# Spreading operands over the partitions by TensorE instead of through DRAM, with a shorter plan at the front

## The chip, the cores and the metric

One core of a Trainium2 chip runs the whole program. The metric is the device time of one execution in microseconds (us). The engines are PE (TensorE; PEld is its weight load), DVE (VectorE), ACT (ScalarE), POOL (GpSimd) and SP (SyncE, which issues nearly all DMAs here). Each works through its own queue in order.

## What is computed

A delta-rule attention over 768 steps for 4 x 8 heads with a 40 x 40 state, then a mixture of experts (one expert of 8 for each of 3072 tokens), then a gated product of two matmuls and an output matmul. The attention, to which the change belongs:

```python
for t in range(S):                     # S = 768, batch 4, 8 heads, D = 40
    y[:, :, t] = np.einsum('bhd,bhde->bhe', rt, state)
    Sa = np.einsum('bhde,bhe->bhd', state, at)
    state_decay = state * wt[:, :, None, :] - np.einsum('bhd,bhe->bhde', Sa, bt)
    state = state_decay + np.einsum('bhd,bhe->bhde', vt, kt)
```

## The kernel before

The 768 steps are split into 12 chunks of 64 (c = 0 to 11). For each chunk some steps, the front, need no state:

- `cum` (L139 to L163): the cumulative products of w in tile `bf`, four scans on DVE (L151).
- `prod` (L165): the inputs `raw` times `bf` (L174, on DVE or POOL), each split into a high and a low float16 part, by ACT and by POOL: `ara` (a), `kb` (k and b), `arr` (r). Each result is stored to DRAM (`out`), as are `bf`'s first two rows (L197, `dg`) and a small decay factor (L205, `dds`).
- `fetch`, `rfetch`: `spread` (L213) reads them back so that the three 40-row groups of the partitions hold the high, low and high parts of the same rows (for a: high, high, low), which lets one 120-row matmul do a product of split numbers. The tiles are `a3`, `kb3`, `r3` (a, kb, r in the rows below) and `DT`.
- `gram` (L256): products of kb and a, one quarter (`g`) at a time, masked into `gm` by DVE (L257). `ztr` transposes kb into Z. `gtr` reads `dg` back into `dl` and transposes it on PE into `gt`, the scale of y.
- `invert` inverts 16 x 16 blocks on DVE, after a trip through DRAM (`tin`, `tl`) that regroups them; `twrite` and `tload` bring the result back by another one (`td`, `TT`); `merge` makes the 64 x 64 inverses out of them on PE, beginning with a transpose on DVE (L298).

The chain then carries the state: for each chunk and each of four blocks, x, u, S and S3 (parts C0 to C4), and the outputs n and y (O0 to O3). Many of these matmuls are float32 and 40 columns wide. Some are preceded by a matmul without use (`warm`, L359).

The source gives every step a due time in `PLAN` (L499): `gram=(5,-1.95,-1.8)` means five pieces that stand between 1.95 and 1.8 chunks ahead of their own. A scheduler then orders each engine's queue when the program is built, from these priorities and its own durations. PSUM tiles of the front steps share one pool, `pb`, with two buffers. The mixture of experts and the last stage follow; their weights begin to load when the last chunks free memory.

Of the kernel before, what the change touches and what calls it, by code (L numbers as in the profile page):

```python
# [10 lines left out]
F32 = mybir.dt.float32  # L11
F32R = mybir.dt.float32r
F16 = mybir.dt.float16
# [4 lines left out]
AF = mybir.ActivationFunctionType  # L18
ALU = mybir.AluOpType
# [4 lines left out]
def sub(ap, off, dims):  # L24

    return bass.AP(tensor=ap.tensor, offset=ap.offset+off, ap=[list(ap.ap[0])]+[list(d) for d in dims])
# [15 lines left out]
    d['vt']=v[:,::-1].reshape(12,128,4*160)[:NC].copy()  # L42
    return d

KB,R3,A3,NZ,GT=1,3,3,4,2
QN,QF=3,3
WARM=(0,256,256,256,256,512,256)
LAG,WHAT=12,'tl'
# [4 lines left out]
class Attn:  # L53
# [13 lines left out]
    def setup1(s):  # L67
        nc=s.nc; c=s.c
        if s.moe is None:
            s.idf=c.tile([128,128],F32,name="idf"); make_identity(nc,s.idf)  # L70
        else: s.idf=s.moe.idf
        s.idh=c.tile([128,128],F16,name="idh"); nc.vector.tensor_copy(s.idh,s.idf)
        s.tri=c.tile([128,64],F32,name="tri"); s.trg=c.tile([128,2,64],F32,name="trg")
        nc.gpsimd.memset(s.tri,1.0)
        for h in (0,1):
            v=s.tri[64*h:64*h+64]
            nc.gpsimd.affine_select(out=v,in_=v,compare_op=ALU.is_gt,fill=0.0,base=0,pattern=[[1,64]],channel_multiplier=-1)
        sc=-1.0/(AL*BE); ts=nc.vector.tensor_scalar
        for p in (0,1):
            ab=slice(64*p,64*p+64); ak=slice(64-64*p,128-64*p)  # L80
            nc.vector.tensor_copy(s.trg[ak,p],s.tri[ak])
            ts(out=s.trg[ab,p],in0=s.tri[ab],scalar1=sc,scalar2=None,op0=ALU.mult)
# [79 lines left out]
        s.load(c+1,0)  # L162
        yield  # L163
    def prod(s,c):
        nc=s.nc; V=nc.vector; d=s.ch[c]; raw=[d[('raw',n)] for n in range(5)]  # L165
        bf=d['bf']
        ar=[s.tile([128,2,6,128],F16,"ar"+n,f"ar{n}{c}",1) for n in "ar"]
        kb=s.tile([128,2,6,2,2,64],F16,"kb",f"kb{c}",KB)
        def out(t,n,w):
            dr=d['d'+n]=s.scr(n,[2,120,6,w],F16,c)  # L170
            nc.sync.dma_start(dr.rearrange("h r i t -> r h (i t)"),t[0:120])
        for (a,o) in ((2,2),(3,2),(1,0)):
            t=raw[a].rearrange("r (i h t) -> r h i t",h=2,t=32)
            (nc.gpsimd if c and a in s.PP else V).tensor_tensor(out=t,in0=t,in1=bf[:,o:o+2,:,o//2:o//2+32],op=ALU.mult)  # L174
            if a==1:
                src=raw[1].rearrange("r (i f) -> r i f",i=6)
                nc.scalar.activation(ar[0][:,0],src,AF.Copy)
                s.psub(ar[0][:,1],src,ar[0][:,0])
                out(ar[0].rearrange("r h i t -> r h (i t)"),"a",128)
            else:  # L180
                o0,ps=((64,64),(0,192))[a-2]
                src=sub(raw[a][:,0:1],0,[[128,6],[64,2],[1,64]])
                d0=sub(kb[:,0,0,0,0,0:1],o0,[[256,6],[ps,2],[1,64]]); d1=sub(kb[:,1,0,0,0,0:1],o0,[[256,6],[ps,2],[1,64]])
                nc.scalar.activation(d0,src,AF.Copy)
                nc.gpsimd.tensor_tensor(out=d1,in0=src,in1=d0,op=ALU.subtract)
                if a==3: out(kb.rearrange("r h i p s t -> r h (i p s t)"),"k",256)
            s.load(c+1,a)
            yield
        src=raw[4].rearrange("r (i f) -> r i f",i=6)
        V.tensor_scalar(out=raw[4],in0=raw[4],scalar1=RO,scalar2=None,op0=ALU.mult)  # L190
        nc.scalar.activation(ar[1][:,0],src,AF.Copy)
        s.psub(ar[1][:,1],src,ar[1][:,0])
        out(ar[1].rearrange("r h i t -> r h (i t)"),"r",128)
        s.load(c+1,4)

        dg=d['dg']=s.scr("g",[120,12,64],F32,c)
        for h in (0,1): nc.sync.dma_start(dg[:,:,32*h:32*h+32],bf[0:120,h,:,0:32])  # L197

        r32=s.tile([128,12],F32,"r32",f"r32{c}",2)
        V.tensor_copy(r32,bf[:,1,:,32])  # L200
        if c>0:
            dd=s.tile([128,12],F32,"dd",f"dd{c}",2); ip='r (i p) -> r i p'
            V.scalar_tensor_tensor(out=dd.rearrange('r (p i) -> r i p',p=2),in0=s.R32.rearrange(ip,p=2),scalar=1.0/(AL*KA),in1=bf[:,2,:,0].rearrange(ip,p=2),op0=ALU.mult,op1=ALU.mult)
            dds=s.dr.tile([2,120,6],F32,tag="dds",name=f"dds{c}")
            nc.sync.dma_start(dds.rearrange("p r i -> r p i"),dd[0:120].rearrange("r (p i) -> r p i",p=2))  # L205
            d['dds']=dds
        s.R32=r32
        d.update(kb=kb)
        yield

    def spread(s,t,dr,lo):
        for g in range(3):
            s.nc.sync.dma_start(t[40*g:40*g+40].rearrange("e (j i) t -> e j (i t)",j=3),dr[int(g==lo)].rearrange("(j e) i t -> e j (i t)",j=3))  # L213
    def rfetch(s,c):
        d=s.ch[c]
        r3=d['r3']=s.tile([128,18,128],F16,"r3",f"r3{c}",R3)
        s.spread(r3,d['dr'],1)
        yield
    def gtr(s,c):
        nc=s.nc; d=s.ch[c]  # L220
        da=s.tile([128,6,2,64],F32,"dl",f"dl{c}",1)
        nc.sync.dma_start(da[0:120].rearrange("r i a t -> r (i a t)"),d['dg'].rearrange("r i t -> r (i t)"))
        gt=d['gt']=s.tile([128,18,40],F32,"gt",f"gt{c}",GT)
        yield
        for hh in (0,1):
            pg=s.pst(f"pg{c}{hh}")
            n=4 if hh==0 else 2
            for i2 in range(n):
                tr=nc.tensor.transpose(pg[:,i2*120:i2*120+120], da[0:120,4*hh+i2].rearrange("p a t -> p (a t)"), s.idf[0:120,0:120])
                if i2==0: s.pin(tr)  # L230
            nc.scalar.activation(sub(gt[:,4*hh,0:1],0,[[240,3],[40,n],[1,40]]),sub(pg[:,0:1],0,[[40,3],[120,n],[1,40]]),AF.Copy)
            yield
    def fetch(s,c):
        nc=s.nc; d=s.ch[c]
        a3=s.tile([128,18,128],F16,"a3",f"a3{c}",A3)
        kb3=s.tile([128,18,2,128],F16,"kb3",f"kb3{c}",1)
        d.update(a3=a3,kb3=kb3)
        s.spread(a3,d['da'],2)
        yield
        s.spread(kb3.rearrange("e k p t -> e k (p t)"),d['dk'],1)  # L240
        yield
        if c>0:
            dds=d['dds']
            for p in (0,1):
                nc.sync.dma_start(s.DT[c%4][64*p:64*p+40].rearrange("e (j i) -> e j i",j=3),dds[p].rearrange("(j e) i -> e j i",e=40))
        yield

    def gram(s,c):
        nc=s.nc; d=s.ch[c]
# [225 lines left out]
        s.load_t(c); yield  # L475
    def run(s):

        for n in (0,2,3,1,4): s.load(0,n)
        ev=[]
        for c in range(s.NC):  # L480
            for nm,(n,a,b) in PLAN.items():
                g=s.part(int(nm[0]=='O'),int(nm[1]),(1,3) if nm=='O3' else range(4),c) if nm[0] in 'CO' else getattr(s,nm)(c)
                for i in range(n): ev.append((c+a+(b-a)*i/n,c,nm,g))
        g1=s.setup2()
        def once(f):
            f(); yield
        ev.append((SETUP[0],-1,'s1',once(s.setup1)))
        if s.moe is not None:
            ev.append((-.8,-1,'s3',once(lambda: s.moe.early_loads(s.tile([128,320],F32,"y","ymoe",2)))))
            ev.append((s.NC-1.4,-1,'s4',once(lambda: s.moe.zero(s.tile([128,320],F32,"y","yzero",2)))))  # L490
        for i in range(6): ev.append((SETUP[1]+i*SETUP[2],-1,'s2',g1))
        ev.sort(key=lambda e:e[0])
        last={}
        for e in ev: last[e[1:3]]=e
        for e in ev:
            next(e[3],0)
            if last[e[1:3]] is e:
                for _ in e[3]: pass
SETUP=(-3.04,-2.3,.05)  # L499
PLAN=dict(cum=(5,-3.456,-2.956),prod=(5,-2.906,-2.556),fetch=(3,-2.45,-2.3),gram=(5,-1.95,-1.8),tread=(1,-1.68,-1.67),ztr=(6,-1.85,-1.5),invert=(30,-1.5,-1.13),twrite=(1,-1.1,-1.09),tload=(1,-0.92,-0.91),gtr=(3,-0.9,-0.3),merge=(9,-0.7,-0.2),vpre=(4,-0.796,-0.088),rfetch=(1,0.05,0.06),C0=(4,-0.081,-0.071),C1=(4,-0.047,0.086),C2=(4,0.191,0.462),O0=(4,0.315,0.573),C3=(4,0.462,0.734),C4=(4,0.463,0.735),O1=(4,0.586,0.858),O2=(4,0.718,0.96),O3=(2,0.96,1.028))  # L500


NT=3072; NTI=24; D=320; E=8; F=1024; FF=1536; NB=13; NBT=21
# [2 lines left out]
class Moe:  # L506
# [463 lines left out]
    def moe2(s,ctx,st):  # L970
# [3 lines left out]
        def fetch(g):  # L974
# [7 lines left out]
            for k in range(3):  # L982
# [3 lines left out]
                s.xsplit(XH,XL,t,k)  # L986
            return XH,XL
        X=fetch(0)
        for g in range(6):
            XH,XL=X  # L990
# [71 lines left out]
```

## Time and profile before

| | us |
|---|---|
| median of 3 runs (lowest, highest) | 1581.28 (1576.04, 1589.54) |
| the profiled execution | 1577.47 |
| its span in the trace | 1575.7 |
| PE busy in the span | 1198.2 |
| DVE, ACT, POOL busy | 716.3, 530.3, 470.9 |

Busy time is the time in which an engine has an instruction under way; matmuls are pipelined, so the mean time of one is longer than its share of a row of them. Idle time of an engine costs something only where the end waits for it. The rows below are copied from the profile's page and from answers of the trace.

### The profile page before, as it was taken

The page shows a single profiled execution, that of the slowest core. Times are in us where ns is not written, and L with a number is a line of the kernel's source. Part 1 is how long each engine was busy: PE and PEld are TensorE (multiplying, and loading weights), DVE is VectorE, ACT ScalarE, POOL GpSimd, SP SyncE. Part 2 cuts the span into 40 slices and gives each one's busy share as a digit, 9 for nine tenths or more (in the row PEclk, how much of TensorE's full clock was granted, in tenths as well). Part 3 has the DMA queues.
Part 4 walks back from the last instruction along what each step waited for, and adds up shares of the span by engine and source line. Part 5 has one row for each costly group of instructions (what it writes and reads, how often), then busy time and mean ns, then how long its engine had stood idle before and what let it go on. Part 6 is the DMA issues. An engine that isn't in the chain of part 4 may idle for free. (4 is left out here: it accounts for less than half of the span.)

```text
span 1575.7 us, 34604 instructions
## 1 busy us (share of the span) xinstructions
PE 1198.2 (76%) x14569; PEld 1043.3 (66%) x14569; DVE 716.3 (45%) x1485; ACT 530.3 (34%) x1068; POOL 470.9 (30%) x434
## 2 busy tenths in 40 slices
PE   0111678955766877698987788887878999999998
PEld 0011567744655666587876687877867888989888
DVE  6552652533333333133324529999989321222211
ACT  5111434321524414343444124545423122131221
POOL 3533421321121301110114206656445232242221
PEclk9999976555756757757765798999989999999999
DMA  6888445454344343423232116777532000100000
GB/s 176 235 211 237 104 128 138 102 150 118 84 111 98 79 105 91 104 63 85 55 104 83 43 45 185 215 213 208 175 95 73 19 18 17 34 9 25 1 17 17
DMA packets 200117, 160.48 MB, mean 102 GB/s; under 512 B 128465, under 2 KB 168209, under 8 KB 199953
## 3 DMA queue, kind: packets, MB, share of 16 engines
q1 hardware_dynamic: 197553, 149.99, 35.8%
q0 software_dynamic: 2400, 8.20, 1.9%
q8 instruction: 116, 1.90, 0.5%
q14 instruction: 48, 0.39, 0.1%
HBM read 113.87 MB, written 44.27 MB: 100 GB/s over the span
## 5 line engine op out<-in xcount | busy, mean ns | idle before, releaser
L807 PE MATMUL ab<-X2H,abh 128*128 128x512 f32 x432 | 171.1, 398 | 4.3 <-DVE pr L997 3.9
L788 POOL TENSOR_TENSOR pL<-pr,pH 128x512 fp32r<-128x512 f32 x72 | 93.4, 1297 | 242.7 <-ACT pH L790 242.5
L807 PE MATMUL ab<-X2H,abl 128*128 128x512 f32 x432 | 121.6, 389 | 0.0
L997 DVE TENSOR_TENSOR pr<-ab,sa 128x512 f32<-128x512 f32 x72 | 49.6, 690 | 149.5 <-PE ab L807 149.5
L807 PE MATMUL ab<-X2L,abh 128*128 128x512 f32 x288 | 112.9, 394 | 0.0
L807 PE MATMUL ph<-XHb,w1h 128*128 128x256 f32 x312 | 89.7, 311 | 29.4 <-DVE hL L874 28.0
L256 PEld LDWEIGHTS <-kb 120*128 120x128 f16 x384 | 25.5, 124 | 130.6 <-issue 117.6
L256 PE MATMUL g<-a,kb 120*128 120x64 f16 x384 | 29.8, 232 | 102.9 <-DMA a<-da 70.7
L807 PEld LDWEIGHTS ab<-X2H,abh 128*128 128x128 f32 x432 | 82.1, 190 | 23.3 <-DVE pr L997 6.1
L790 ACT ACTIVATE pH<-pr 128x512 fp32r<-128x512 f32 x72 | 45.6, 633 | 144.0 <-DVE pr L997 132.4
L807 PEld LDWEIGHTS ab<-X2H,abl 128*128 128x128 f32 x432 | 81.1, 188 | 16.9
L1007 PE MATMUL po<-wol,pH 128*128 128x320 f32 x288 | 89.7, 312 | 1.5 <-POOL wol L788 1.5
L1007 PE MATMUL po<-woh,pH 128*128 128x320 f32 x288 | 89.5, 312 | 0.2 <-ACT woh L951 0.2
L788 POOL TENSOR_TENSOR w1l<-wr,w1h 128x512 fp32r<-128x512 f32 x51 | 71.1, 1408 | 59.9 <-ACT w1h L828 38.1
L1007 PE MATMUL po<-woh,pL 128*128 128x320 f32 x288 | 88.8, 311 | 0.0
L807 PEld LDWEIGHTS ph<-XHb,w1h 128*128 128x128 f32 x312 | 65.2, 210 | 35.6 <-DVE hL L874 29.5
L120 POOL TENSOR_TENSOR Q<-Qf,Q 128x320 f16<-128x320 f32 x48 | 38.0, 793 | 150.5 <-ACT Q L428 150.5
L996 ACT ACTIVATE sa<-ab 128x512 f32<-128x512 f32 x72 | 43.0, 597 | 113.5 <-PE ab L807 113.0
L174 POOL TENSOR_TENSOR raw<-raw,bf 128x768 f32<-128x768 f32 x22 | 38.8, 1764 | 131.8 <-DVE bf L151 48.0
L377 PE MATMUL x<-Qf,gm 64*64 64x40 f32 x768 | 57.2, 292 | 20.1 <-DVE Qf L354 20.1
L151 DVE TENSOR_TENSOR_SCAN bf<-raw,D 128x396 f32<-128x396 f32 x48 | 51.1, 1085 | 39.9 <-DMA dg<-bf 31.0
L884 PE MATMUL po<-w2h,hH 128*128 128x320 f32 x208 | 65.8, 319 | 2.9 <-ACT hH L873 2.9
(309 smaller groups left out, 3238.4 us busy)
## 6 DMA issues: line engine op xcount, KB each, us to landing
raw<-ct SPq DMA_DIRECT2D x48, 384.0 KB
kb<-dk SPq DMA_DIRECT2D x36, 360.0 KB
wr<-moe_w SPq DMA_DIRECT2D x40, 320.0 KB
wr<-moe_w SPq DMA_DIRECT2D x40, 256.0 KB
dk<-kb SPq DMA_DIRECT2D x12, 720.0 KB
a<-da SPq DMA_DIRECT2D x36, 180.0 KB
r<-dr SPq DMA_DIRECT2D x36, 180.0 KB
wr<-moe_w SPq DMA_DIRECT2D x40, 128.0 KB
```

Source lines behind the costliest of these rows:

```text
L120: def psub(s,out,a,b): s.nc.gpsimd.tensor_tensor(out=out,in0=a,in1=b,op=ALU.subtract)
L151: V.tensor_tensor_scan(o,i,d1.rearrange("p i t -> p (i t)"),0.0,ALU.mult,ALU.add)
L174: (nc.gpsimd if c and a in s.PP else V).tensor_tensor(out=t,in0=t,in1=bf[:,o:o+2,:,o//2:o//2+32],op=ALU.mult)
L256: nc.tensor.matmul(pg[:,(q*2+p)*64:(q*2+p)*64+64], d['kb3'][0:120,k,p], d['a3'][0:120,k,64*p:64*p+64], start=True,stop=True)
L377: mm(o(px,q,p),gm[r,k0+q,p],Q[r,p,q],start=not S,stop=not S or q==3)
L788: def psub(s,L,a,H): s.nc.gpsimd.tensor_tensor(out=L,in0=a,in1=H,op=ALU.subtract)
L790: s.nc.scalar.activation(H,src,AF.Copy)
L807: for i,(a,b) in enumerate(l): mm(o,a,b,start=(i==0),stop=(i==7))
L884: nc.tensor.matmul(po,a[:,m,tk],b[:,m],start=(k==0 and m==0 and n==0),stop=(k==3 and m==1 and n==2))
L996: sa=w.tile([128,512],F32,tag="sa",name=f"sa{g}{m}"); nc.scalar.activation(sa,pp[0],AF.Copy)
L997: pr=w.tile([128,512],F32,tag="pr",name=f"pr{g}{m}"); V.tensor_tensor(out=pr,in0=pp[1],in1=sa,op=ALU.mult)
L1007: nc.tensor.matmul(po,a[:,m,tk],b[:,m],start=(n==0),stop=(n==35)); n+=1
```

## The change

The stores of `ara`, `kb`, `arr`, `bf` and the decay factor and all reads of them are gone. In their place `spread` multiplies the stored halves by a constant selection matrix `sps` (two accumulating matmuls for a piece of up to 512 columns, first the high and then the low part) into a `pb` buffer, and ACT and DVE take turns in copying the piece to `kb3`, `a3` or `r3`. `gtr` regroups `bf` by a copy on POOL and transposes that. The decay factor is brought to its partitions by six small float32 matmuls. The scaling and splitting of r moves out of `prod` into `rprep`, 0.3 chunks ahead of the chunk's own time, and `r3` has one buffer instead of three. In the plan `cum` begins 2.75 chunks ahead instead of 3.456, `gtr` moves to the front, and the steps from `gram` on keep their times.

```diff
-KB,R3,A3,NZ,GT=1,3,3,4,2
+KB,R3,A3,NZ,GT=1,1,3,4,4
...
+        s.sps=c.tile([128,2,2,3,120],F16,name="sps"); nc.gpsimd.memset(s.sps,0.0)
+        for y,lo in ((0,2),(1,1)):
+            for g in range(3):
+                nc.vector.tensor_copy(s.sps[:,y,int(g==lo),:,40*g:40*g+40],s.idh[:,0:120].rearrange("p (j e) -> p j e",j=3))
...
-            nc.sync.dma_start(dr.rearrange("h r i t -> r h (i t)"),t[0:120])
...
-        dg=d['dg']=s.scr("g",[120,12,64],F32,c)
-        for h in (0,1): nc.sync.dma_start(dg[:,:,32*h:32*h+32],bf[0:120,h,:,0:32])
...
-            nc.sync.dma_start(dds.rearrange("p r i -> r p i"),dd[0:120].rearrange("r (p i) -> r p i",p=2))
+            pd=s.pst(f"pd{c}")
+            for j in range(3):
+                for p in (0,1): nc.tensor.matmul(pd[64*p:64*p+40,6*j:6*j+6],s.idf[0:120,40*j:40*j+40],dd[0:120,6*p:6*p+6],start=True,stop=True)
+            for p in (0,1): nc.scalar.activation(s.DT[c%4][64*p:64*p+40],pd[64*p:64*p+40,0:18],AF.Copy)
...
-    def spread(s,t,dr,lo):
-        for g in range(3):
-            s.nc.sync.dma_start(t[40*g:40*g+40].rearrange("e (j i) t -> e j (i t)",j=3),dr[int(g==lo)].rearrange("(j e) i t -> e j (i t)",j=3))
+    def spread(s,dst,src,y,w,nm):
+        nc=s.nc; n0=512//w; n=0
+        for j in range(3):
+            m=6 if j<2 else 4; st=n0 if m%n0==0 else 3
+            for i in range(0,m,st):
+                ps=s.pst(f"sp{nm}{j}{i}"); o=ps[0:120,0:st*w]
+                for h in (0,1): nc.tensor.matmul(o,s.sps[0:120,y,h,j],src[0:120,h,i:i+st].rearrange("r i t -> r (i t)"),start=h==0,stop=h==1)
+                d=dst[0:120,6*j+i:6*j+i+st]; o=o.rearrange("r (i t) -> r i t",i=st)
+                if n%2: nc.vector.tensor_copy(d,o)
+                else: nc.scalar.activation(d,o,AF.Copy)
+                n+=1
+                yield
...
-        nc.sync.dma_start(da[0:120].rearrange("r i a t -> r (i a t)"),d['dg'].rearrange("r i t -> r (i t)"))
+        nc.gpsimd.tensor_copy(da.rearrange("r i p (h t) -> r h (i p) t",h=2),bf[:,0:2,:,0:32])
...
-PLAN=dict(cum=(5,-3.456,-2.956),prod=(5,-2.906,-2.556),fetch=(3,-2.45,-2.3),gram=(5,-1.95,-1.8),tread=(1,-1.68,-1.67),ztr=(6,-1.85,-1.5),invert=(30,-1.5,-1.13),twrite=(1,-1.1,-1.09),tload=(1,-0.92,-0.91),gtr=(3,-0.9,-0.3),merge=(9,-0.7,-0.2),vpre=(4,-0.796,-0.088),rfetch=(1,0.05,0.06),C0=(4,-0.081,-0.071),C1=(4,-0.047,0.086),C2=(4,0.191,0.462),O0=(4,0.315,0.573),C3=(4,0.462,0.734),C4=(4,0.463,0.735),O1=(4,0.586,0.858),O2=(4,0.718,0.96),O3=(2,0.96,1.028))
+PLAN=dict(cum=(5,-2.75,-2.56),gtr=(3,-2.55,-2.35),prod=(4,-2.5,-2.26),spr=(13,-2.25,-1.97),gram=(5,-1.95,-1.8),tread=(1,-1.68,-1.67),ztr=(6,-1.85,-1.5),invert=(30,-1.5,-1.13),twrite=(1,-1.1,-1.09),tload=(1,-0.92,-0.91),merge=(9,-0.7,-0.2),vpre=(4,-0.796,-0.088),rprep=(1,-0.3,-0.29),rspr=(5,0.06,0.3),C0=(4,-0.081,-0.071),C1=(4,-0.047,0.086),C2=(4,0.191,0.462),O0=(4,0.315,0.573),C3=(4,0.462,0.734),C4=(4,0.463,0.735),O1=(4,0.586,0.858),O2=(4,0.718,0.96),O3=(2,0.96,1.028))
```

In the rows that follow a name ends with the piece, the chunk and a serial number: `tin0_355` is chunk 0's tin, `kb31` chunk 1's kb3, `raw23` input 2 of chunk 3, `spk310` a piece of k's spread for chunk 3, `x10` the x of chunk 1, block 0.

On SP, in the fill, these stand from the first chunk's tin to its read tl, before:

```order
L263 DMA tin0_355<-gm0_282 16x16x16 x8
L213 DMA kb31_424<-dk1_351 40x3x1536 x3
L133 DMA raw23_505<-ct 128x768
L171 DMA dk2_548<-kb2_501 120x2x1536
L133 DMA raw33_550<-ct 128x768
L245 DMA DT2_218<-dds2_619 40x3x6
L213 DMA a31_423<-da1_369 40x3x768 x3
L171 DMA dr2_608<-arr2_500 120x2x768
L133 DMA raw43_610<-ct 128x768
L245 DMA DT2_218<-dds2_619 40x3x6
L213 DMA r31_1845<-dr1_389 40x3x768
L269 DMA tl0_364<-tin0_355 128x256
```

and these now:

```order
L138 DMA raw03_741<-wt 128x794
L138 DMA raw22_437<-ct 128x768
L138 DMA raw32_453<-ct 128x768
L264 DMA tin0_378<-gm0_320 16x16x16 x8
L138 DMA raw12_467<-ct 128x768
L270 DMA tl0_387<-tin0_378 128x256
```

Ten rows between tin0 and tl0 became one, a load.

On DVE, ahead of the first transpose of the first merge, before:

```order
L174 TENSOR_TENSOR raw34_1081<-raw34_1081,bf4_1449 128x2x12x32
L190 TENSOR_SCALAR raw44_1156<-raw44_1156 128x768
L151 SCALAR_TENSOR_TENSOR bf5_2308<-raw05_1667,D0_127 128x396 x2
L157 RECIPROCAL rr5_2309<-bf5_2308 128x12
...
L159 TENSOR_SCALAR D1_128<-rr5_2309 128x12
L151 SCALAR_TENSOR_TENSOR bf5_2308<-raw05_1667,D1_128 128x396
L174 TENSOR_TENSOR raw35_1935<-raw35_1935,bf5_2308 128x2x12x32
L298 STREAM_TRANSPOSE T11_209<-TT0_207 128x512
```

and now:

```order
L212 CAST kb32_971<-spk222_1017 120x512
L156 SCALAR_TENSOR_TENSOR bf4_2152<-raw04_1373,D1_145 128x396
L164 TENSOR_SCALAR D1_145<-rr4_2153 128x12
L212 CAST a32_970<-spa203_1069 120x384
L156 SCALAR_TENSOR_TENSOR bf4_2152<-raw04_1373,D1_145 128x396
L299 STREAM_TRANSPOSE T11_201<-TT0_199 128x512
```

Before, the scans of chunks 0 to 5 (24), eight products and five scalings of r stand ahead of that transpose; now it is the scans of chunks 0 to 4 (20), six products, two scalings and 17 evictions of spreads.

On PE, in the x step of chunk 1, before:

```order
L373 MATMUL x10_1690<-S300_1383,a31_423 64x40
L256 LDWEIGHTS kb33_1454
L256 MATMUL g131_1874<-a33_1453,kb33_1454 128x64
...
L359 LDWEIGHTS sel_270
L359 MATMUL g132_1896<-sel_270 128x512
...
L377 MATMUL x10_1690<-Qf10_1458,gm1_475 64x40
L330 MATMUL p110_1413<-TT1_208,P1b0_210 64x32 x16
```

and now:

```order
L378 MATMUL x10_1860<-Qf10_1575,gm1_564 64x40 x5
L210 LDWEIGHTS sps_127
L210 MATMUL spk310_1805<-kb3_1511,sps_127 120x512
L210 LDWEIGHTS sps_127
L210 MATMUL spk310_1805<-kb3_1511,sps_127 120x512
L378 MATMUL x10_1860<-Qf10_1575,gm1_564 64x40 x3
L371 LDWEIGHTS zh_298
L371 MATMUL x11_1880<-sel_296,zh_298 128x160
L374 LDWEIGHTS a31_493
```

Where pieces of chunk 3's gram stood between the matmuls of x, pairs of chunk 3's spread stand now, and its gram comes behind x. All spreads of k and a for chunks 0 to 2 stand ahead of the first merge's matmuls or just behind their first ones.

## Rows read from the trace of the kernel before

**Rows 1.** The page's 40 slices of the span: PE busy, granted clock, in tenths.
```profile
PE   0111678955766877698987788887878999999998
PEclk9999976555756757757765798999989999999999
```
**Rows 2.** Answers by tile: min/median/max ns, then first and last start in us.
```profile
L257 DVE TENSOR_TENSOR gm<-g,trg x48: 630/692/693, 51.2 to 729.0; 128x512 f32<-128x512 f32 x48
L276 DVE TENSOR_TENSOR tA<-tl,I x12: 382/383/1662, 87.3 to 766.3; 128x256 f32<-128x256 f32 x12
L298 DVE STREAM_TRANSPOSE T<-TT x12: 699/702/711, 142.2 to 801.5; 128x512 f32<-128x512 f32 x12
L453 DVE SCALAR_TENSOR_TENSOR y<-y,gt x48: 308/325/327, 230.8 to 871.3; 128x160 f32<-128x160 f32 x48
```
**Rows 3.** Stretches: length, busy us of PE, PEld, DVE, ACT, POOL; granted clock; DMA share; GB/s.
```profile
0.00:142.00 142.00, 11.43 (x140) 7.70 (x140) 72.98 (x141) 38.32 (x52) 54.60 (x43) 1.00 0.79 207
142.00:872.00 730.00, 553.16 (x10768) 464.08 (x10768) 273.21 (x720) 273.95 (x606) 162.15 (x183) 0.67 0.42 104
735.00:872.00 137.00, 118.78 (x2153) 100.02 (x2152) 48.34 (x135) 59.57 (x133) 35.95 (x52) 0.63 0.30 82
560.00:600.00 40.00, 37.69 (x537) 32.10 (x537) 12.19 (x45) 12.56 (x31) 3.41 (x5) 0.50 0.34 73
526.00:541.00 15.00, 12.16 (x228) 9.91 (x226) 2.37 (x6) 10.17 (x23) 4.11 (x6) 0.96 0.29 62
1300.00:1350.00 50.00, 50.00 (x247) 42.78 (x246) 10.67 (x16) 14.47 (x25) 14.60 (x12) 1.00 0.06 15
```
**Rows 4.** Waits from 0 to 142 us: who for whom, us in total, times, longest.
```profile
PE g L256 <- DMA a<-da: 70.7, 2, 45.7
DVE raw L174 <- DMA raw<-ct: 17.8, 2, 10.3
DVE bf L151 <- DMA dg<-bf: 14.7, 1, 14.7
```
**Rows 5.** The same from 142 to 872 us.
```profile
ACT arr L191 <- DMA dr<-arr: 48.7, 3, 19.5
DVE raw L190 <- DMA raw<-ct: 40.8, 4, 18.5
PE g L256 <- DMA kb<-dk: 27.8, 3, 11.7
PE S L359 <- ACT Qf L389: 16.5, 1, 16.5
```
**Rows 6.** Groups by line over the span: busy us, mean ns | idle before.
```profile
L151 DVE TENSOR_TENSOR_SCAN bf<-raw,D 128x396 f32<-128x396 f32 x48 | 51.1, 1085 | 39.9 <-DMA dg<-bf 31.0 <-POOL raw L174 5.3 <-DMA raw<-wt 3.3
L996 ACT ACTIVATE sa<-ab 128x512 f32<-128x512 f32 x72 | 43.0, 597 | 113.5 <-PE ab L807 113.0 <-ACT pH L790 0.4
L257 DVE TENSOR_TENSOR gm<-g,trg 128x512 f32<-128x512 f32 x48 | 32.6, 687 | 55.6 <-PE g L256 55.2
L359 PE MATMUL g<-sel 128*128 128x512 f16 x48 | 26.0, 549 | 18.8 <-DVE gm L257 11.8 <-DVE sel L113 3.9 <-ACT Z L343 2.1
L581 PE MATMUL lg<-wgt,xt 128*128 128x8 f32 x96 | 22.3, 342 | 0.7 <-ACT xt L578 0.7
L174 DVE TENSOR_TENSOR raw<-raw,bf 128x768 f32<-128x768 f32 x14 | 20.5, 1474 | 21.3 <-DMA raw<-ct 17.8 <-ACT kb L184 3.3
L1008 DVE COPY yo<-po 128x320 f32<-128x320 f32 x24 | 11.7, 491 | 104.4 <-PE po L1007 104.4
L190 DVE TENSOR_SCALAR raw<-raw 128x768 f32<-128x768 f32 x12 | 7.6, 635 | 59.5 <-DMA raw<-ct 59.5
```
**Rows 7.** The chain that ended last: start us, us, what.
```profile
1307.79 32.67 PE ab L807 x144
```
**Rows 8.** PE's groups from 560 to 600 us, and then from 526 to 541 us.
```profile
L386 PE MATMUL u<-X,TT 64*64 64x40 f32 x64 | 4.3, 307 | 0.0
L386 PE MATMUL u<-X,TT 64*64 64x40 f32 x48 | 2.3, 229 | 0.0
```

More of the change, by code (lines that the diff above doesn't have):

```diff
@@ L164, in prod @@
     def prod(s,c):
-        nc=s.nc; V=nc.vector; d=s.ch[c]; raw=[d[('raw',n)] for n in range(5)]
+        nc=s.nc; V=nc.vector; d=s.ch[c]; raw=[d[('raw',n)] for n in range(4)]
         bf=d['bf']
-        ar=[s.tile([128,2,6,128],F16,"ar"+n,f"ar{n}{c}",1) for n in "ar"]
+        ar=s.tile([128,2,6,128],F16,"ara",f"ara{c}",1)
         kb=s.tile([128,2,6,2,2,64],F16,"kb",f"kb{c}",KB)
-        def out(t,n,w):
-            dr=d['d'+n]=s.scr(n,[2,120,6,w],F16,c)
-            nc.sync.dma_start(dr.rearrange("h r i t -> r h (i t)"),t[0:120])
+        d.update(kb=kb,ar=ar)
         for (a,o) in ((2,2),(3,2),(1,0)):
@@ L176, in prod @@
                 src=raw[1].rearrange("r (i f) -> r i f",i=6)
-                nc.scalar.activation(ar[0][:,0],src,AF.Copy)
-                s.psub(ar[0][:,1],src,ar[0][:,0])
-                out(ar[0].rearrange("r h i t -> r h (i t)"),"a",128)
+                nc.scalar.activation(ar[:,0],src,AF.Copy)
+                s.psub(ar[:,1],src,ar[:,0])
             else:
@@ L185, in prod @@
                 nc.gpsimd.tensor_tensor(out=d1,in0=src,in1=d0,op=ALU.subtract)
-                if a==3: out(kb.rearrange("r h i p s t -> r h (i p s t)"),"k",256)
             s.load(c+1,a)
             yield
[L189 to L194, printed above, removed]
-        dg=d['dg']=s.scr("g",[120,12,64],F32,c)
-        for h in (0,1): nc.sync.dma_start(dg[:,:,32*h:32*h+32],bf[0:120,h,:,0:32])
         r32=s.tile([128,12],F32,"r32",f"r32{c}",2)
@@ L203, in prod @@
             V.scalar_tensor_tensor(out=dd.rearrange('r (p i) -> r i p',p=2),in0=s.R32.rearrange(ip,p=2),scalar=1.0/(AL*KA),in1=bf[:,2,:,0].rearrange(ip,p=2),op0=ALU.mult,op1=ALU.mult)
-            dds=s.dr.tile([2,120,6],F32,tag="dds",name=f"dds{c}")
-            nc.sync.dma_start(dds.rearrange("p r i -> r p i"),dd[0:120].rearrange("r (p i) -> r p i",p=2))
-            d['dds']=dds
+            pd=s.pst(f"pd{c}")
+            for j in range(3):
+                for p in (0,1): nc.tensor.matmul(pd[64*p:64*p+40,6*j:6*j+6],s.idf[0:120,40*j:40*j+40],dd[0:120,6*p:6*p+6],start=True,stop=True)
@@ L207, in prod @@
+            for p in (0,1): nc.scalar.activation(s.DT[c%4][64*p:64*p+40],pd[64*p:64*p+40,0:18],AF.Copy)
         s.R32=r32
-        d.update(kb=kb)
         yield
-    def spread(s,t,dr,lo):
-        for g in range(3):
-            s.nc.sync.dma_start(t[40*g:40*g+40].rearrange("e (j i) t -> e j (i t)",j=3),dr[int(g==lo)].rearrange("(j e) i t -> e j (i t)",j=3))
[L214 to L217, printed above, removed]
+    def spread(s,dst,src,y,w,nm):
[10 more added lines that the diff above has]
+                yield
@@ L218, in rfetch, with rprep, rspr @@
+    def rprep(s,c):
+        nc=s.nc; raw=s.ch[c]['raw',4]
+        rr=s.ch[c]['rr']=s.tile([128,2,6,128],F16,"arr",f"arr{c}",1)
+        src=raw.rearrange("r (i f) -> r i f",i=6)
+        nc.vector.tensor_scalar(out=raw,in0=raw,scalar1=RO,scalar2=None,op0=ALU.mult)
+        nc.scalar.activation(rr[:,0],src,AF.Copy)
+        s.psub(rr[:,1],src,rr[:,0])
+        s.load(c+1,4)
         yield
+    def rspr(s,c):
+        r3=s.ch[c]['r3']=s.tile([128,18,128],F16,"r3",f"r3{c}",R3)
+        yield from s.spread(r3,s.ch[c]['rr'],1,128,f"r{c}")
@@ L219, in gtr @@
     def gtr(s,c):
-        nc=s.nc; d=s.ch[c]
+        nc=s.nc; d=s.ch[c]; bf=d['bf']
         da=s.tile([128,6,2,64],F32,"dl",f"dl{c}",1)
-        nc.sync.dma_start(da[0:120].rearrange("r i a t -> r (i a t)"),d['dg'].rearrange("r i t -> r (i t)"))
+        nc.gpsimd.tensor_copy(da.rearrange("r i p (h t) -> r h (i p) t",h=2),bf[:,0:2,:,0:32])
+        yield
         gt=d['gt']=s.tile([128,18,40],F32,"gt",f"gt{c}",GT)
-        yield
         for hh in (0,1):
@@ L228, in gtr, with spr @@
             for i2 in range(n):
-                tr=nc.tensor.transpose(pg[:,i2*120:i2*120+120], da[0:120,4*hh+i2].rearrange("p a t -> p (a t)"), s.idf[0:120,0:120])
-                if i2==0: s.pin(tr)
+                nc.tensor.transpose(pg[:,i2*120:i2*120+120], da[0:120,4*hh+i2].rearrange("p a t -> p (a t)"), s.idf[0:120,0:120])
             nc.scalar.activation(sub(gt[:,4*hh,0:1],0,[[240,3],[40,n],[1,40]]),sub(pg[:,0:1],0,[[40,3],[120,n],[1,40]]),AF.Copy)
             yield
-    def fetch(s,c):
-        nc=s.nc; d=s.ch[c]
+    def spr(s,c):
+        d=s.ch[c]
         a3=s.tile([128,18,128],F16,"a3",f"a3{c}",A3)
@@ L237, in fetch @@
         d.update(a3=a3,kb3=kb3)
[L238 to L246, printed above, removed]
+        yield from s.spread(kb3.rearrange("e k p t -> e k (p t)"),d['kb'].rearrange("r h i p s t -> r h i (p s t)"),1,256,f"k{c}")
+        yield from s.spread(a3,d['ar'],0,128,f"a{c}")
     def gram(s,c):
@@ L476, in run @@
     def run(s):
-        for n in (0,2,3,1,4): s.load(0,n)
+        for n in (0,2,3,1): s.load(0,n)
         ev=[]
@@ L487, in run @@
         ev.append((SETUP[0],-1,'s1',once(s.setup1)))
+        ev.append((-1.7,-1,'s5',once(lambda: s.load(0,4))))
         if s.moe is not None:
```

## The prediction

> **What bounds the kernel now.** I read the slices of the span first, to see where TensorE (PE) idles and at which granted clock [rows 1]. PE does almost nothing in the first four slices, is then busy for 55 to 90% at a clock of mostly 0.5 to 0.7 until about slice 22, and nearly full at 0.9 or more behind it. The change touches the attention alone, and the last y tile ends at 871 us [rows 2]; everything after it (704 us) I carry over unchanged.
>
> The stretches [rows 3] cut the attention in two. From 0 to 142 us PE is busy for 11.43 us: this is the fill, which ends with the first transpose of the merge at 142.2 us [rows 2]. From 142 to 872 us PE is busy for 553.16 of 730 us, 0.758 of the time, while DVE, ACT and POOL have 273, 274 and 162 us. So PE is the engine that limits this part, with 177 us of waiting in it. In the last stretch, where no front work is left, its share is 118.78 of 137, 0.867; from 560 to 600 us it is 0.942, at half clock.
>
> Who was waited for comes third. In the fill [rows 4] PE waits 70.7 us for tile a on its way back from DRAM, in two pieces; DVE waits 17.8 us for raw inputs at the products and 14.7 us because `bf` can't be overwritten before its copy to DRAM is out. From 142 us on [rows 5] PE waits 27.8 us for kb from DRAM and 16.5 us behind ACT, whose queue stood 48.7 us in all at `arr`, an operand still being written out; DVE stood 40.8 us at the scaling of r.
>
> **The change part by part.**
>
> *DRAM trips removed.* Per chunk the writes of a, k, r, g and dds and their reads go; the waits in the last paragraph that name da, dk, dr and dg go with them. The raw loads and the four trips of the inversion (tin, tl, td, TT) stay.
>
> *The fill.* In before 91 us lie between the first gram result (51.2 us) and the merge (142.2 us), with the first inversion at 87.3 us [rows 2]. The order of SP shows why a part of that can go: between tin0 and its read tl0 stood spreads, operand stores and loads; one load is left. DVE is what remains. Ahead of its first merge transpose it drops four scans (x 1.085), three scalings of r (x 0.635) and two products (x 1.474), 9.2 us in all, and gets 17 evictions of spreads and six small copies [rows 6]. DVE shows no eviction of a 120x512 spread: it lies between 0.491 us (a 128x320 copy from PSUM) and 0.687 us (the 128x512 gram result from PSUM); I take 0.65, nearer the row of that width. That is 11.1 us, with 1 us for the small copies (an estimate). DVE's busy time until the merge goes from 72.98 to 75.9 us. I add the 17.8 us of waiting for raw inputs at products, which stay, and drop the others: 94 us, a saving of 48 us. Bounds: if all of the 91 us stays behind a gram at 45 us, the merge starts at 136 us (6 saved); if DVE never waits, at 76 (66 saved).
>
> *PE's new work.* A chunk's spreads are 16 matmuls of 512 columns for k, and 8 of 384 and 2 of 512 each for a and r: 16384 columns, as much as 32 matmuls of 512. Those of k and a for chunks 0 to 2 (order of PE) stand ahead of the first merge, where PE idles anyway. Behind it are left 9 chunks of k and a and 12 of r, 312 matmuls of 512. Back to back such a matmul takes 32.67/144 = 0.227 us [rows 7] in a stretch with a granted clock of 1.00 [rows 3]: 70.8 us. The upper end is the warming matmul of the same width, 0.549 us from start to end [rows 6]: 171 us. At the clock of this stretch, 0.67, it is 70.8/0.67 = 106 us, which I take, since these matmuls stand among the others. The small product for the decay, 6 float32 matmuls a chunk of 6 columns, has no row; the nearest is the 128x8 float32 one with 0.342 us [rows 6], and below it nothing where the pieces overlap. I take 0.2 us x 54 = 11 us. g's transposes were there before. PE's busy time after the merge: 553 + 106 + 11 = 670 us.
>
> *ACT, DVE, POOL.* Eighteen evictions a chunk, ten on ACT at 0.597 us (128x512 from PSUM [rows 6]) and eight on DVE at 0.65, are 72 and 62 us over twelve chunks; with 274 and 273 of 730 us they stay under half. POOL's copy of g, 128x768, lies on an engine that is busy for 162 of 730 us. I cost these at nothing in the sum: PE's time covers them. If the cover is gone, PE waits for a free `pb` buffer (there are two), and this is a rival.
>
> *The clock.* The same matmul u takes 307 ns at a granted clock of 0.50 and 229 ns at 0.96 [rows 8, 3], so a stretch at the full level (2.4 GHz instead of 1.2) costs a quarter less. From 560 to 600 us PE is busy for 94% and still has the half level, with narrow float32 matmuls (40 columns) as its main work; at 526 to 541 us, with 81%, it has the full one. How far spreads of 512 columns lift it no row of before shows. Bounds: nothing, and 0.85 as the mean. I take a small step, 0.67 to 0.73: half-level time goes from 0.66 to 0.54 of it, 0.12 x 670 x 0.25 = 20 us less, 650 us. The Trainium skill ("TensorE: Matmul & The Clock Gate", Part 1) says that the throttled clock is the default and activity releases it. By that, dense spreads lift it more than I take, and the time is that of the first rival; the 94% busy stretch at 0.50 shows that being busy alone doesn't do it.
>
> *The waiting that is left.* PE's share was 0.867 where nothing came through DRAM for it and no filler was left. Now spreads of a chunk ahead stand between x, u and y (order of PE), and they need no result of the step before. I take 0.88, a little over the tail and under the 0.942: 650/0.88 = 739 us.
>
> *Sum.* 94 + 739 = 833 us to the end of the attention, against 872: 39 us less. The profiled execution took 1577.5 us, so 1538; it lies 3.8 us under the median of 1581.3, and I say **1540 us**.
>
> **Rivals.**
>
> *The clock rises.* With a mean of 0.85 the half level has 0.30 of the time instead of 0.66: 0.36 x 670 x 0.25 = 60 us less, 610/0.88 + 94 = 787, 85 us under before: 1493 us. For it: dense f16 columns are the new work, 14.5 us of them at the half level in a chunk of some 60 us. Against it: they stand in pairs among the same narrow matmuls.
>
> *Given back.* PE gets 117 us more work and nothing is filled: at the tail's 0.867 and an unchanged clock 670/0.867 + 94 = 867 us, 5 under before, 1573 us. With the fill hardly shorter (136 us) and 0.88 it is 650/0.88 + 136 = 875, 1581 us. The trips were then hidden by the front that ran ahead. For it: of the 177 us in which PE waits, the two waits above are only 44. Against it: the fill's 131 idle us are in the rows.
>
> *Slower: evictions hold PE.* Every spread needs a free `pb` buffer, and ACT and DVE take the eviction in their order, behind chain steps that themselves wait for PE. Each chunk has 18 such pieces where gram and its transposes had 9. Break-even is a PE share of 670/(872 - 94) = 0.861 at the old clock, just below the tail's, and at 0.844 the kernel is 1% slower. Half way between 0.867 and the 0.758 of before, 0.81, it is 827 + 94 = 921 us, 49 more: 1627 us. The Trainium skill ("TensorEngine Tiling (Array Packing)", PSUM Bottleneck) warns that evacuation may become the bottleneck when TensorE does more, and advises using both engines, as is done here. For the rival: ACT's queue already stood still for tens of us. Against: most of that was at `arr`'s store, which goes.
>
> **How the numbers follow.** Forecast (1515 to 1565 us) 0.40; the clock rises 0.20; given back 0.18; slower 0.22. About 1% is what a measurement of this kernel can tell from no change, so faster (under 1565) has 0.60, the same 0.18, slower (over 1597) 0.22. The range must hold the rising clock and the milder half of the slower case: 1478 to 1620, which leaves out some 0.06 below and 0.12 above.
>
> **What would show it.** Right: the first merge transpose starts between 76 and 110 us; no wait of PE for kb or a by DMA; PE busy about 650 us behind the merge at a clock over 0.7 and a share of 0.86 to 0.92; the last y at about 833 us; 704 us behind it. The clock rival shows as a mean granted clock over 0.8 there; the given-back one as a merge after 125 us, or a share at 0.867 with the clock at 0.67; the slower one as PE waiting at the spread matmuls for ACT or DVE, tens of us in total. I am wrong outright if PE's idle time moves to a wait that I don't name, such as the raw loads, which now come fewer chunks ahead, or the inversion's trips.

## The result, and the profile after

The changed kernel takes **1498.74 us** (median, 1491.13 to 1501.97) against 1582.74 of the kernel before on the same chip, a ratio of 0.946 with a 95% interval of 0.941 to 0.952: 84 us faster. The forecast was 1540 with a range of 1478 to 1620. The direction and the range hold; the gain is twice the 41 us that were forecast (1581 to 1540), and it is near the time of the rival in which the clock rises (1493).

The page's slices of the changed kernel, in the columns of [rows 1]:

```profile
PE   2678988969999797799988877778698999999998
PEclk9756586975757798797656989999899999999999
```

The empty slices at the left are gone, and the stretch of the attention has more digits of 7 to 9 in its clock than [rows 1], with 5 and 6 still between them.

First and last starts of four instructions, by tile:

```profile
L258 DVE TENSOR_TENSOR gm<-g,trg x48: 677/692/693, 44.8 to 679.5; 128x512 f32<-128x512 f32 x48
L277 DVE TENSOR_TENSOR tA<-tl,I x12: 381/404/1217, 57.1 to 692.2; 128x256 f32<-128x256 f32 x12
L299 DVE STREAM_TRANSPOSE T<-TT x12: 680/711/712, 92.5 to 729.0; 128x512 f32<-128x512 f32 x12
L454 DVE SCALAR_TENSOR_TENSOR y<-y,gt x48: 285/325/326, 160.0 to 794.2; 128x160 f32<-128x160 f32 x48
```

Against [rows 2] the first merge starts at 92.5 instead of 142.2 us, and the last y comes at 794 instead of 871. Between gram and the first inversion lie 12 us instead of 36, and from there to the merge 35 instead of 55.

The stretches, with the columns of [rows 3] (length, busy us of PE, PEld, DVE, ACT, POOL, granted clock, DMA share, GB/s):

```profile
0.00:92.00 92.00, 43.40 (x254) 24.79 (x255) 68.79 (x149) 44.57 (x73) 40.86 (x37) 0.84 0.39 98
92.00:795.00 703.00, 623.04 (x11219) 479.03 (x11217) 295.48 (x814) 327.40 (x728) 183.88 (x198) 0.72 0.25 61
795.00:1500.00 705.00, 629.84 (x3663) 567.37 (x3661) 376.64 (x626) 218.44 (x410) 258.86 (x212) 0.96 0.27 79
```

Of the 77 us by which the attention is shorter, 50 are the fill and 27 the part behind the merge. PE does 70 us more in that part (623 against 553) and still ends it sooner, since it waits for 80 us there instead of 177. What follows the attention takes 705 us against 704.

The waits behind the merge, as in [rows 5]:

```profile
POOL raw L177 <- DMA raw<-ct: 67.0, 11, 11.1
DVE T L299 <- DMA TT<-td: 66.0, 9, 14.2
ACT kb L213 <- PE spk L210: 54.0, 17, 6.0
DVE r L212 <- PE spr L210: 39.1, 16, 6.4
PE g L360 <- DVE gm L258: 23.7, 3, 10.2
```

No DMA stands among the long waits of PE any more. The DMAs that are waited for are the raw loads and the inversion's trips, by POOL and DVE. At the spreads the evicting engines wait for PE; PE itself has no wait ahead of a spread matmul there. Its largest wait, 23.7 us in all at gram (`g`) for the mask `gm` by DVE, is one that the prediction doesn't name.

### The profile page after: what moved, and what is told of

Its sections match the earlier page's. It is cut to its first block, busy times and chain, and to the rows that moved or that the text cites. A ratio compares the mean times of both kernels' runs of the same rounds, so it can differ in the third digit from the quotient of the medians.

```text
span 1500.2 us, 35616 instructions
## 1 busy us (share of the span) xinstructions
PE 1296.3 (86%) x15133; PEld 1071.2 (71%) x15133; DVE 740.9 (49%) x1587; ACT 590.4 (39%) x1210; POOL 483.6 (32%) x447
## 5 line engine op out<-in xcount | busy, mean ns | idle before, releaser
L210 PEld LDWEIGHTS <-sps 120*120 120x120 f16 x432 | 58.4, 165 | 58.8 <-issue 48.0
L210 PE MATMUL spk<-kb,sps 120*120 120x512 f16 x192 | 74.8, 502 | 25.9 <-POOL kb L187 9.3
L125 POOL TENSOR_TENSOR Q<-Qf,Q 128x320 f16<-128x320 f32 x48 | 42.9, 895 | 95.8 <-ACT Q L429 89.1
L187 POOL TENSOR_TENSOR kb<-raw,kb 128x768 f16<-128x768 f32 x24 | 40.7, 1718 | 89.8 <-ACT kb L186 77.1
L334 POOL MEMSET TT<- 32x512 f32 x24 | 12.5, 521 | 177.1 <-PE p L331 138.4
L809 PE MATMUL ph<-XLb,w1h 128*128 128x256 f32 x208 | 57.6, 303 | 10.4 <-DVE XLb L861 10.4
```

Of the source, the lines that this page charges most:

```text
L125: def psub(s,out,a,b): s.nc.gpsimd.tensor_tensor(out=out,in0=a,in1=b,op=ALU.subtract)
L210: for h in (0,1): nc.tensor.matmul(o,s.sps[0:120,y,h,j],src[0:120,h,i:i+st].rearrange("r i t -> r (i t)"),start=h==0,stop=h==1)
L809: for i,(a,b) in enumerate(l): mm(o,a,b,start=(i==0),stop=(i==7))
```

## The experiments

Two theories were left to tell apart for the part behind the merge: that a spread costs its columns at the clock as it is (columns), and that dense columns raise the clock and pay for themselves (clock). For the fill it was the path (no trips) against the plan (a front that runs less far ahead). The first four kernels below share their runs of the kernel before; so do the next four, and so do the last three. Across these groups the ratio to the kernel before compares better than the times do.

### The plan without the path

```diff
-cum=(5,-3.456,-2.956),prod=(5,-2.906,-2.556),fetch=(3,-2.45,-2.3)
+cum=(5,-2.75,-2.56),prod=(5,-2.5,-2.26),fetch=(3,-2.25,-1.97)
```

> The kernel before with the shorter plan alone: cum, prod and fetch get the due times of the changed kernel, operands still go through DRAM. Theory path (the trips were what was waited for; the plan only orders DVE's queue): the first merge moves from 142 to between 115 and 135 us, PE waits longer than 28 us for kb and a by DMA behind it, and the time is 1560 to 1610 us. Rival plan (the gain comes from a front that no longer runs six chunks ahead): merge at about 95 us, 1500 to 1530 us.

It took 1560.5 us, ratio 0.991 (0.988 to 0.995). The first merge, by tile, and PE's and ACT's longest waits for DMAs behind it:

```profile
L298 DVE STREAM_TRANSPOSE T<-TT x12: 698/711/712, 143.1 to 780.6; 128x512 f32<-128x512 f32 x12
...
ACT arr L191 <- DMA dr<-arr: 45.0, 4, 13.0
PE g L256 <- DMA kb<-dk: 15.5, 2, 13.6
PE g L256 <- DMA dr<-arr: 8.5, 1, 8.5
```

The time lies in the range of theory path, the mechanism does not: the merge doesn't move at all (143.1 us), and the waits for kb don't grow. DVE's wait for raw inputs at the products of the fill stays too (18.5 us, 17.8 in [rows 4]). The plan alone is worth about 1%, all of it behind the merge.

### The path without the plan

```diff
-cum=(5,-2.75,-2.56),gtr=(3,-2.55,-2.35),prod=(4,-2.5,-2.26),spr=(13,-2.25,-1.97)
+cum=(5,-3.456,-2.956),gtr=(3,-2.95,-2.85),prod=(4,-2.906,-2.556),spr=(13,-2.45,-2.0)
```

> The changed kernel with the front's old due times (cum from 3.456, prod from 2.906, spreads from 2.45 chunks ahead; gtr follows cum). Theory path: trips stay away, so the part behind the merge keeps its length (700 us, PE share 0.88); the first merge comes later, at 105 to 130 us, since DVE takes scans of more chunks first: 1510 to 1540 us. Rival plan: 1560 us or more.

It took **1454.0 us**, ratio 0.923 (0.917 to 0.930), less than either theory allowed and less than the changed kernel itself. By tile the first merge starts at 91.6 us. The part behind it:

```profile
92.00:748.00 656.00, 577.67 (x11198) 449.76 (x11199) 305.02 (x809) 325.56 (x722) 189.27 (x198) 0.77 0.25 64
```

So the 50 us of the fill come from the path alone: 143 us with the trips, 92 without them, whatever the plan. My expectation that an earlier front would hold up the merge was wrong. And the shorter plan costs time on the new path: behind the merge it has the same work and the same share of PE (0.881 here, 0.886 there), but a clock of 0.72 instead of 0.77.

### Each spread matmul twice

```diff
-for h in (0,1): nc.tensor.matmul(o,...,start=h==0,stop=h==1)
+for h in (0,1,0,1): nc.tensor.matmul(o,...,start=h==0,stop=h==1)
```

> The changed kernel with each spread matmul done twice into the same PSUM buffer (the second pair starts the sum anew), evictions unchanged. Theory columns (PE limits, a spread costs its columns at the clock as it is): 312 more matmuls of 512 behind the merge are 71 us at the full clock, 98 at 0.72, 111 at PE's share of 0.886: 1600 to 1620 us with a granted clock of 0.70 to 0.74 behind the merge. Rival clock (dense columns raise the clock and so pay for themselves in part): granted clock over 0.78 there, 1520 to 1570 us.

It took 1520.3 us, ratio 0.965 (0.959 to 0.971), 21.5 more than the changed kernel. The whole stretch, and then the spreads' own rows in it (PE, PEld):

```profile
92.00:804.00 712.00, 624.40 (x11605) 472.90 (x11605) 303.61 (x825) 332.88 (x732) 191.29 (x203) 0.85 0.24 61
...
92.00:804.00 712.00, 202.41 (x748) 98.85 (x748) 0.85 0.24 61
```

and the spreads' rows of the changed kernel:

```profile
92.00:795.00 703.00, 128.98 (x357) 44.39 (x355) 0.72 0.25 61
```

The spreads take 73 us more, and PE as a whole 1 us more (624.4 against 623.0): everything else on PE became 72 us shorter, with the clock at 0.85. This is the rival clock, at the lower end of its range. PE now waits at the spreads, too, for a `pb` buffer that DVE has yet to empty:

```profile
PE spa L210 <- DVE kb L212: 35.0, 6, 6.8
```

So the two buffers, which hold PE nowhere at the spreads of the changed kernel, do so here.

### PE's new work without its use, in the kernel before

```diff
+    def dmy(s,c):
+        for i in range(16):
+            ps=s.pst(f"dm{c}{i}")
+            for h in (0,1): s.nc.tensor.matmul(ps,s.sel[0:120,4],s.sel[0:120,0:4].rearrange("p a b -> p (a b)"),start=h==0,stop=h==1)
+            yield
...
+dmy=(16,0.06,0.9),
```

> The kernel before with PE's new work alone: 16 pairs of matmuls of 512 columns per chunk into pb buffers, spread over the chunk's own time, without use, evictions or any change of path or plan. Theory columns: 384 matmuls are 87 us at the full clock and 130 at 0.67, and about half of it fits into PE's 177 us of waiting: 1630 to 1690 us, clock at 0.67 to 0.70 from 142 us to the attention's end. Rival clock: the clock goes over 0.75 there and the time stays under 1610 us.

It took 1536.9 us, ratio 0.975 (0.969 to 0.982): work without use makes the kernel before 41 us faster.

```profile
143.00:829.00 686.00, 592.05 (x11136) 440.47 (x11136) 258.22 (x708) 276.89 (x604) 157.16 (x179) 0.81 0.43 110
```

The trips and the fill are as in [rows 3]; the clock goes from 0.67 to 0.81, and PE waits for 94 us instead of 177. The added matmuls alone (PE):

```profile
143.00:829.00 686.00, 134.21 (x384) 0.81 0.43 110
```

They take 134 us of PE, and the rest of its work 458 instead of 553.

The control has the same matmuls with 40 columns instead of 512:

```diff
-nc.tensor.matmul(ps,s.sel[0:120,4],s.sel[0:120,0:4]...
+nc.tensor.matmul(ps[:,0:40],s.sel[0:120,4],s.sel[0:120,0,0:40],...
```

> The kernel before with the same 384 added matmuls, but 40 columns wide instead of 512, so that PE gets the instructions and the scheduler's new order and hardly any columns. Theory clock (dense columns raise PE's clock): the granted clock behind the merge falls back to 0.66 to 0.70 and the time to 1570 to 1600 us. Rival order (the added matmuls helped because the scheduler put the other rows in another order): 1530 to 1550 us as with 512 columns, clock as it may.

It took 1586.8 us, ratio 1.000 (0.996 to 1.004):

```profile
144.00:884.00 740.00, 565.77 (x11149) 474.63 (x11150) 259.77 (x720) 275.62 (x604) 162.21 (x183) 0.67 0.41 102
```

The gain is gone and the clock is back at 0.67. It was the columns, not the instructions or the slots that they took in the queue. The scheduler's order differs somewhat between the two, so the last few us are not told apart.

### Each eviction twice

```diff
+for _ in (0,1):
     if n%2: nc.vector.tensor_copy(d,o)
     else: nc.scalar.activation(d,o,AF.Copy)
```

> The changed kernel with each spread piece copied out of PSUM twice by the same engine. Theory cover (PE's time covers the evictions): 18 more copies a chunk, about 7 us on ACT and 5 on DVE of some 58 us, 1495 to 1515 us. Rival evictions (PE is held by the two pb buffers): each piece holds its buffer 0.6 us longer, 216 pieces: 1540 to 1620 us, with PE waiting for tens of us more at the spreads.

Its median is 1490.3 us (1474.0 to 1500.2), not over the changed kernel's. The stretch behind the merge, and the longest wait of PE for a spread's buffer:

```profile
93.00:774.00 681.00, 627.69 (x11240) 478.18 (x11240) 345.53 (x912) 380.91 (x840) 185.54 (x201) 0.77 0.26 63
...
PE spk L210 <- DVE kb L213: 5.0, 1, 5.0
```

ACT and DVE do 54 and 50 us more there, and PE's waits ahead of spread matmuls come to some 8 us, not to tens. The rival in which evictions hold PE falls for this kernel. That they cost nothing is not shown: the clock behind the merge is 0.77 here and 0.72 in the changed kernel, PE is busy for 628 us all the same, and what the higher clock gave may hide what the evictions cost.

### Why the old due times are faster on the new path

Two kernels split what the second one had changed: the lead of `cum`, `gtr` and `prod`, and the span over which the spreads stand.

```diff
 # lead_only
+cum=(5,-3.456,-2.956),gtr=(3,-2.95,-2.85),prod=(4,-2.906,-2.556),spr=(13,-2.25,-1.97)
 # spr_wide
+cum=(5,-2.95,-2.76),gtr=(3,-2.75,-2.55),prod=(4,-2.7,-2.46),spr=(13,-2.45,-2.0)
```

> The changed kernel with cum, gtr and prod at the old, earlier due times, but the spreads at the new, narrow ones (2.25 to 1.97 chunks ahead). Theory placement (the kernel with the old due times is faster because its spreads stand over 0.45 of a chunk instead of 0.28, which keeps the clock up): 1485 to 1505 us, clock behind the merge 0.71 to 0.74. Rival lead (the earlier front takes late waits away from PE): 1450 to 1470 us, with a clock near 0.72 and a PE share over 0.90.

> The changed kernel with cum, gtr and prod only 0.2 chunks earlier than in it, so that the spreads can stand over 2.45 to 2.0 chunks ahead. Theory placement: 1450 to 1470 us with a clock behind the merge of 0.75 to 0.79. Rival lead: 1485 to 1505 us.

The first took 1480.1 us, ratio 0.940 (0.933 to 0.948), the second **1451.8**, ratio 0.921 (0.913 to 0.928). The parts behind the merge, of the first:

```profile
91.00:774.00 683.00, 589.07 (x11208) 461.43 (x11207) 304.14 (x812) 328.46 (x726) 184.95 (x198) 0.75 0.25 62
```

and of the second:

```profile
92.30:739.50 647.20, 552.07 (x11198) 428.58 (x11195) 289.35 (x801) 327.07 (x728) 180.84 (x198) 0.81 0.27 65
```

A wide span with a short lead gives the lowest time and the highest clock of the kernels with this work; a long lead with a narrow span lies between it and the changed kernel. So the span of the spreads is the larger part, as theory placement said, though both clocks lie above those that it gave (0.71 to 0.74 and 0.75 to 0.79); the lead gives something too, less than the rival said. What it is in the new order that keeps the clock up isn't settled: the due times move hundreds of rows on PE, and single executions of the wide kernel differ by 24 us. The granted clock over the whole span goes with them, in one and the same program: 0.881 and 0.880 at 1440 and 1443 us, 0.860 and 0.857 at 1461 and 1464.

### Can more columns still pay?

> The kernel with the spreads over 2.45 to 2.0 chunks ahead once more, beside the two below. 1440 to 1465 us, with a clock behind the merge of 0.78 to 0.82.

> The kernel with the wide spreads and all its warming matmuls 512 columns wide instead of mostly 256, which adds 5120 columns a chunk without a new instruction, wait or buffer. Theory clock: a mean of 0.86 or more behind the merge; the columns, 26 us at the full clock, are paid back: 1425 to 1450 us. Rival columns (above a mean of 0.8 more columns cost what they are): 1465 to 1485 us.

```diff
-WARM=(0,256,256,256,256,512,256)
+WARM=(0,512,512,512,512,512,512)
```

> The kernel with the wide spreads and 6 pairs of useless 512-column matmuls a chunk, due 0.2 to 0.6 chunks into it, where no spread of k or a stands: 6144 columns a chunk, 31 us at the full clock. Theory clock: a mean of 0.86 or more, 1425 to 1455 us. Rival columns: 1470 to 1490 us.

```diff
+        for i in range(6):
...
+dmy=(6,0.2,0.6),
```

On one chip the three took 1458.4 us, ratio 0.918 (0.913 to 0.923); 1462.0, ratio 0.923 (0.919 to 0.928); and 1494.7, ratio 0.942 (0.937 to 0.947). Wider warming columns are neither a gain nor a loss that these runs tell, and the time lies between the ranges of the two theories. The granted clock over the whole span is 0.884 to 0.895 in five of its six executions (1450 to 1466 us) and 0.864 in the sixth (1487 us); without the wider columns it is 0.853 to 0.882. So the clock is a little higher with the wider columns, and they about pay for themselves. The six pairs cost 36 us, 5 more than the upper end of rival columns allowed. Their stretch, then the pairs alone (PE) and PE's longest wait:

```profile
92.00:786.00 694.00, 606.12 (x11371) 449.51 (x11368) 299.89 (x818) 331.32 (x733) 182.36 (x202) 0.81 0.26 63
...
92.00:786.00 694.00, 51.51 (x144) 0.81 0.26 63
...
PE g L360 <- DVE gm L258: 48.6, 7, 11.1
```

The clock stays where it was without them, 0.81, so the columns are paid in full: the pairs take 51.5 us and the rest of PE's work 555, against 552 without them. PE's waits come to 88 us against 95; the longest, for gram's mask on DVE, is 49 us here and 30 without the pairs. Here theory clock fails. The wide kernel without additions stays the best: 1452 and 1458 us as the medians of its two sets of runs, 8% under before.

## Why the prediction was right or wrong

**The fill: right in size, half right in its parts.** Forecast was the merge at 94 us; it starts at 92.5. DVE is busy for 68.8 us, not 75.9, and waits for 23, not 17.8. The evictions cost what I took:

```profile
L212 DVE CAST kb<-spk 120x512 f16<-120x512 f32 x12 | 8.2, 685 | 10.0 <-PE spk L210 10.0
L177 DVE TENSOR_TENSOR raw<-raw,bf 128x768 f32<-128x768 f32 x6 | 6.1, 1038 | 2.1 <-DMA raw<-ct 2.1
```

These are groups of DVE in the first 92 us of the changed kernel (busy, mean ns | idle before). The 512-wide eviction takes 0.685 us there (forecast 0.65). The products take 1.04 us instead of the 1.474 of [rows 6]. They wait 2.1 us for raw inputs and not 17.8, which I had carried over as staying: that wait went with the trips, since it is 18.5 us in the kernel with the plan alone and 2.1 in the one with the path alone. The DMA engines are busy for 0.39 of the fill instead of 0.79 ([rows 3]). In its place DVE waits for the spreads, 10.0 us at k's. That the sum came out within 2 us is in part luck. That it is the path which shortens the fill, and not the plan, is shown by the two kernels that have one without the other.

**PE's new work: right as a sum.** I put PE's busy time behind the merge at 670 us at the clock of before. Busy time multiplied by the granted clock gives 670 x 0.67 = 449 us at the full level; the trace gives 623 x 0.72 = 449. That the two agree to the microsecond is in part luck, since the parts don't: the spreads' own rows take 129 us where 106 were forecast, and the rest of PE's work 494 where 564 were.

**The clock's step: right in size, wrong in what it is worth.** I forecast 0.67 to 0.73 and the rows show 0.72. But I counted 20 us for it, from one matmul's start-to-end time at the two levels (307 and 229 ns, [rows 8]). These times contain a part that runs beside the next matmul: the 64 matmuls of [rows 8] take 307 ns each from start to end, but 4.3 us together, 67 ns each. What the level costs shows in the changed kernel, in a stretch at a granted clock of 0.50 (333.1 to 387.6 us) and one at 1.00 (575.5 to 616.2 us), with equal counts:

```profile
L210 PE MATMUL spk<-kb,sps 120*120 120x512 f16 x16 | 8.3, 649 | 0.0
L378 PE MATMUL x<-Qf,gm 64*64 64x40 f32 x64 | 5.6, 309 | 0.0
L450 PE MATMUL y<-Z,nf 128*64 128x40 f32 x64 | 5.0, 308 | 0.0
...
L210 PE MATMUL spk<-kb,sps 120*120 120x512 f16 x16 | 4.6, 391 | 0.0
L378 PE MATMUL x<-Qf,gm 64*64 64x40 f32 x64 | 3.1, 230 | 0.0
L450 PE MATMUL y<-Z,nf 128*64 128x40 f32 x64 | 3.0, 230 | 0.0
```

From start to end a matmul x or y is a quarter shorter at the full level, as I took it. In PE's busy time the three rows go from 18.9 to 10.7 us, 43% less. So a microsecond at the half level does 0.57 of the work of one at the full level, and the step from 0.67 to 0.73 gives 670 x (0.66 x 0.57 + 0.34)/(0.54 x 0.57 + 0.46) = 625 us, an estimate: 45 less, not 20. A simpler rule puts PE's busy time at the inverse of the mean clock: 670 x 0.67/0.73 = 615 us, 55 less. With it the sum would have been 615/0.88 + 94 = 793 us, and the time 1577.5 - 79 = 1498; with 625 it would have been about 1510. The price of the level is the step that failed, and it is most of the difference. The table shows the simpler rule on the profiled executions whose rows stand above:

| kernel | PE busy behind the merge, us | clock | product | profiled execution, us |
|---|---|---|---|---|
| before | 553 | 0.67 | 371 | 1577 |
| before, pairs of 40 columns | 566 | 0.67 | 379 | 1588 |
| before, pairs of 512 columns | 592 | 0.81 | 480 | 1537 |
| changed | 623 | 0.72 | 449 | 1502 |
| changed, long lead | 589 | 0.75 | 442 | 1478 |
| changed, old due times | 578 | 0.77 | 445 | 1451 |
| changed, wide spreads | 552 | 0.81 | 447 | 1440 |
| changed, wide spreads and six pairs | 606 | 0.81 | 491 | 1488 |
| changed, matmuls twice | 624 | 0.85 | 531 | 1514 |
| changed, evictions twice | 628 | 0.77 | 483 | 1483 |

The product stands for the work: it is 442 to 449 for the four kernels that do the same. Over 0.72 to 0.81 it can't tell a price of a half from one of 43%. It rises by 78 from before to changed (71 were forecast for the spreads at the full level) and by 82 where the spreads are doubled. Elsewhere the rule is rough. The 384 useless matmuls of 512 columns add 109 in the kernel before, where their columns are 87 at the full level, and the six pairs add 44 to the wide kernel for 33. The kernel with doubled evictions does the changed kernel's matmuls and has 483; 21 more of its spread matmuls stand behind the merge (378, not 357), which is 5 us, and the rest is open.

**PE's share: right.** Forecast 0.88, measured 623/703 = 0.886.

**The rivals.** *The clock rises* was put at 0.20 and is, as a mechanism, what happened, at less than its mean of 0.85 but at a better price for each step. That its time of 1493 is 6 us from the result is luck: the step was smaller than it took (0.72, not 0.85) and each part of it worth more. Against it I had said that the spreads stand in pairs among narrow matmuls; the pairs of 512 columns in the kernel before are just that, and take it from 0.67 to 0.81. The Trainium skill ("TensorE: Matmul & The Clock Gate", Part 1) has it that activity releases the throttled clock; the pairs of 512 columns agree (0.67 to 0.81), while those of 40 columns, which are activity too, left it at 0.67. *Given back* falls: PE waits for 97 us less. *Evictions hold PE* falls for the changed kernel, with no wait of PE ahead of its spreads and some 8 us with the evictions doubled. Such waits do appear in other kernels: 36 us where the spreads are doubled, and 20 to 25 us in the three with other due times.

**What I treated as one and was two.** The path and the plan pull in opposite directions. The path with the old due times gains 124 us; the plan on top of it loses 45 by the medians, some 36 by the two ratios (0.923 and 0.946). Nothing in the forecast priced the plan behind the merge, and the profile of before would have given a hint only by its clock.

## What to carry to other kernels

Where TensorE is the engine that limits a stretch and its granted clock is well under 1, price its work as busy time times clock, as a first estimate, and an edit by what it does to both: in the kernel before, dense columns that replaced waiting were cheaper than free. Test that with useless matmuls before building the real thing; one run with 512 columns and one with 40 tells columns from order. And split a change that moves work and due times into the two, since one may hide what the other costs.

## What the runs showed that I had not expected

- 384 useless matmuls of 512 columns made the kernel before 41 us faster (0.975, 0.969 to 0.982). The effect ends: at a clock of 0.81, 144 more in the wide kernel left it at 0.81 and cost 36 us.
- Due times alone move the mean clock of the same work from 0.72 to 0.81, and the time by 47 us by the medians (some 40 by the ratios).
- Doubling 216 PSUM evictions did not lengthen the kernel (1490 against 1499 us), at a clock of 0.77 behind the merge instead of 0.72, which nothing here explains.
